# Second layer of a two-layer kernel: splits of transposed activations queued behind the next normalizations, and the last tiles' transposes behind their step's products

## The chip, the cores and the metric

One core of one Trainium2 chip runs the whole program. The core has five engines that run side by side, each in the order of its own instruction queue: PE (TensorE, matrix products), DVE (VectorE), ACT (ScalarE), POOL (GpSimd) and SP (SyncE, which here only issues DMAs). The metric is the device time in microseconds (us) of one execution; lower is better.

## What is computed

Attention over a window of 64 keys makes `x` (2304 tokens of 512 values); two layers follow. The change touches the second:

```python
h = x @ w_in                                  # 2304 x 512 times 512 x 1024
e = np.exp(h - h_max)
sm = e / (np.sum(e, axis=-1, keepdims=True) + 1e-09)
solu = h * sm
mu = np.mean(solu, axis=-1, keepdims=True)
var = np.mean((solu - mu) ** 2, axis=-1, keepdims=True)
ln = (solu - mu) / np.sqrt(var + 1e-06) * g_ln
return (ln @ w_out).astype(np.float32)        # 2304 x 1024 times 1024 x 512
```

## The kernel before

Every float32 operand of a product is held as two parts, hi and lo, and a product is three matmuls: hi with hi, hi with lo, lo with hi.

The second layer walks over 18 tiles of 128 tokens, t0 to t17. For a tile:

- `st_h2` (matmuls on L605): 24 matmuls of 512 columns make 1024 values a token in PSUM, tile `ps_h2`, of which there are three buffers.
- `st_ln`: the softmax-like unit and the normalization. The chain is DVE max (L616), ACT exponential (L617), three DVE steps (L618 to L620; L620 is the last to read `ps_h2`), DVE L621, ACT square with its sum (L622), DVE L623, POOL power (L624), DVE L628. The tiles `e` and `s` have two buffers each.
- `st_move`, all but the last three tiles: DVE transposes blocks of 32x32 (L638), SP writes the tile to DRAM (`lnd`, L639, 512 KB) and reads it back turned, in four pieces of 128 KB (`lT`, L641). A DRAM buffer is written and landed before it is read, so this is a round trip.
- `st_t2`: for both halves of the turned tile, ACT casts the hi part (`wih`, L662) and DVE subtracts it to get the lo part (`wil`, L663). The pair of casts and subtractions is called the splits here. The last three tiles (`DIRECT`) don't go through DRAM: PE turns them with 8 transposes (L657) into a `ps_h2` buffer and the splits read that.
- `st_out`: 24 matmuls (L674) into `ps_o` (two buffers), an ACT copy (L680), and a DMA out. The last tile does it in two halves of 256 columns.

`x2_split` makes hi and lo of the layer's input, three tiles at a time (ACT L525, DVE L526), from `x2r`, which a DMA of 768 KB loads (L516).

The loop runs 22 steps with `LAG = 4`: step i has the first product of tile i and the second of tile i-4. A scheduler then sorts each engine's instructions by its own estimate of time, so that the text order is a wish and not the queue's order; the instructions' dependencies and the order between calls named in the text are kept. In the text of before, `st_t2` of the last three tiles stands ahead of `st_out` of its step, and `st_t2` of the others stands at the end of the step with nothing that holds it back.

Below, "out k" is the second product of tile k, and "lnd k", "lT k" and "splits of k" go by tile in the same way.

Of the kernel before, what the change touches and what calls it, by code (L numbers as in the profile page):

```python
# [11 lines left out]
ACTF = mybir.ActivationFunctionType  # L12
ALU = mybir.AluOpType
# [7 lines left out]
def kernel(  # L21
# [12 lines left out]
    nc = tc.nc  # L34
# [63 lines left out]
    def as_f32(a):  # L98
        return a.bitcast(F32)
# [51 lines left out]
    def wtile(tag):  # L151
        return w_p.tile([128, 512], F32R, tag=tag, name=tag)
# [251 lines left out]
    def moe_g2(ps, u, hi, lo):  # L404
        g = nc.vector.tensor_tensor(u, ps, u, op=ALU.max)  # L405
        return nc.scalar.copy(hi, u).ins, g.ins  # L406
# [104 lines left out]
    NI = NT // 128  # L511
    x2h, x2l, x2raw = {}, {}, {}

    def x2_load(j):
        r = d_p.tile([128, KC, NB], F32, tag="x2", bufs=1, name="x2r")
        nc.sync.dma_start(out=r, in_=x2d[j].rearrange("e p n -> p e n"))  # L516
        x2raw[j] = r

    def x2_split(j, es):
        r = x2raw[j]  # L520
        if 0 in es:
            x2h[j] = wk_p.tile([128, KC, NB], F32R, tag="xh", name="x2h")
            x2l[j] = wk_p.tile([128, KC, NB], F32R, tag="xl", name="x2l")
        for e in es:
            nc.scalar.copy(x2h[j][:, e, :], r[:, e, :])  # L525
            nc.vector.tensor_tensor(  # L526
                x2l[j][:, e, :], r[:, e, :], as_f32(x2h[j][:, e, :]), op=ALU.subtract
            )
# [4 lines left out]
    for n in range(len(seq) + 2):  # L533
        if n < len(seq):
# [3 lines left out]
            if c == FIRST:  # L538
                z = na * (f + 1) // F0 - na * f // F0
# [18 lines left out]
        if n < len(seq):  # L558
# [3 lines left out]
            pins = moe_g2(*part)  # L562
# [32 lines left out]
    def st_h2(i):  # L595
        j, t = divmod(i, TPN)
        ps = ps2.tile([128, DF2], F32, tag="h2", bufs=3, name="ps_h2")
        tc_ = slice(t * 128, t * 128 + 128)
        for nn in range(2):
            cs = slice(nn * 512, nn * 512 + 512)  # L600
            n = 0
            for kc in range(KC):
                hi, lo = x2h[j][:, kc, tc_], x2l[j][:, kc, tc_]
                for a, w in ((hi, w2ih), (hi, w2il), (lo, w2ih)):
                    nc.tensor.matmul(ps[:, cs], a, w[kc, nn], start=(n == 0), stop=(n == 3 * KC - 1))  # L605
                    n += 1
        h2[i] = ps

    def st_ln(i):
        ps = h2.pop(i)  # L610
        e = d_p.tile([128, DF2], F32, tag="e", name="e")
        s = d_p.tile([128, DF2], F32, tag="s", name="s")
        l_ = s
        st = d_p.tile([128, 8], F32, tag="stat", name="stat")
        nmx, sm, rs, ssum, nmu, vs, rstd = (st[:, z:z + 1] for z in range(7))
        nc.vector.reduce_max(nmx, ps, axis=mybir.AxisListType.X, negate=True)  # L616
        nc.scalar.activation(e, ps, ACTF.Exp, bias=nmx, scale=1.0, accum_out=sm)  # L617
        nc.vector.tensor_scalar(sm, sm, 1e-9, None, op0=ALU.add)  # L618
        nc.vector.reciprocal(rs, sm)
        nc.vector.scalar_tensor_tensor(s, ps, rs, e, op0=ALU.mult, op1=ALU.mult, accum_out=ssum)  # L620
        nc.vector.tensor_scalar(nmu, ssum, -1.0 / DF2, None, op0=ALU.mult)  # L621
        nc.scalar.activation(e, s, ACTF.Square, bias=nmu, scale=1.0, accum_out=vs)  # L622
        nc.vector.tensor_scalar(vs, vs, 1.0 / DF2, 1e-6, op0=ALU.mult, op1=ALU.add)  # L623
        nc.gpsimd.tensor_tensor(rstd, vs, mhalf, op=ALU.pow)  # L624
        if i in DIRECT:
            l_ = e.rearrange("p (k b i) -> p b k i", b=4, i=32)
            s = s.rearrange("p (b k i) -> p b k i", b=4, i=32)
        nc.vector.tensor_scalar(l_, s, nmu, rstd, op0=ALU.add, op1=ALU.mult)  # L628
        ln[i] = l_, e

    def st_move(i):
        l_, lt = ln[i]
        if i not in DIRECT:
            lT = d_p.tile([128, 4, NK2, 32], F32, tag="st", bufs=NST, name="lT")
            nc.vector.transpose(lt, l_)  # L638
            nc.sync.dma_start(out=lnd[i], in_=lt)  # L639
            for a in range(4):  # L640
                nc.sync.dma_start(  # L641
                    out=lT[:, a].rearrange("p k j -> p (k j)"),
                    in_=lnd[i][32 * a:32 * a + 32, :].rearrange("i (b m) -> b i m", b=4),
                )
            ln[i] = lT

    def st_t2(i):
        lnh[i], lnl[i] = {}, {}
        l_ = ln.pop(i)
        for a in range(2):  # L650
            hi, lo = wtile(f"wih{8 + 2 * (i % 2) + a}"), wtile(f"wil{8 + 2 * (i % 2) + a}")
            lnh[i][a], lnl[i][a] = (z.rearrange("p (k t) -> p k t", t=128) for z in (hi, lo))
            if i in DIRECT:
                if a == 0:
                    ps = ps2.tile([128, DF2], F32, tag="h2", bufs=3, name="ps_t2")
                    for c in range(0, DF2, 128):
                        nc.tensor.transpose(ps[:, c:c + 128], l_[1][:, c:c + 128], ident)  # L657
                src = ps[:, 512 * a:512 * a + 512]
            else:
                src = l_[:, :, 4 * a:4 * a + 4, :].rearrange("p a k j -> p k a j")  # L660
                hi, lo = (z.rearrange("p (k a j) -> p k a j", k=4, a=4) for z in (hi, lo))
            nc.scalar.copy(hi, src)  # L662
            nc.vector.tensor_tensor(lo, src, as_f32(hi), op=ALU.subtract)  # L663


    def st_out(i):
        hi, lo = lnh.pop(i), lnl.pop(i)
        w = DM // 2 if i == NI - 1 else DM
        for c in range(0, DM, w):
            ps = ps2.tile([128, DM], F32, tag="o", name="ps_o")[:, 0:w]  # L670
            n = 0
            for kk in range(NK2):
                for a, b in ((hi, w2oh), (hi, w2ol), (lo, w2oh)):
                    nc.tensor.matmul(  # L674
                        ps, a[kk // 4][:, kk % 4, :], b[kk][:, c:c + w],
                        start=(n == 0), stop=(n == 3 * NK2 - 1),
                    )
                    n += 1
            o = d_p.tile([128, DM], F32, tag="o", name="o")[:, 0:w]
            nc.scalar.copy(o, ps)  # L680
            nc.sync.dma_start(out=out[i * 128:(i + 1) * 128, c:c + w], in_=o)

    LAG = 4
    for i in range(NI + LAG):
        if i < NI:
            st_h2(i)
        if i - 2 in DIRECT:
            st_t2(i - 2)  # L690
        if i >= LAG:
            st_out(i - LAG)
        if i < NI:
            st_ln(i)
            st_move(i)
            j, t = divmod(i, TPN)
            if t < 2 and j + 1 < NBLK:
                x2_split(j + 1, (2 * t, 2 * t + 1))
            if t == 2 and j + 2 < NBLK:
                x2_load(j + 2)  # L700
        for z in sorted(ln):
            if z <= i - LAG + 1 and z not in DIRECT:
                st_t2(z)


# [28 lines left out]
```

## Time and profile before

| | us |
|---|---|
| median of 3 runs | 748.56 |
| lowest and highest of them | 747.93 and 750.5 |
| the profiled execution | 749.73 |
| its span, first to last instruction | 747.9 |
| PE busy in it | 718.5 |
| DVE, ACT, POOL busy | 459.7, 355.1, 142.9 |

The profile is of one execution. The second layer's first matmul starts 530.74 us after the start of the span. A view that lists instructions gives start, duration, engine, line and operation, output and inputs, how many were merged, and in brackets how long the engine sat idle before and what it waited for. PE's matmuls overlap: the distance from start to start is their pace, not the duration shown.

### The profile page before, as it was taken

The numbers are of one execution on the slowest core, as the hardware profiler recorded it, in microseconds if no ns is written. First come the engines' busy times: TensorE is split into PE (matmuls) and PEld (weight loads), VectorE is DVE, ScalarE is ACT, GpSimd is POOL, SyncE is SP. The second block draws the span as 40 slices with busy tenths as digits, with TensorE's granted clock in tenths as the row PEclk, the third lists the DMA queues.
The fourth block names the chain that finished last, engine by engine and source line by source line (L and its number), as shares of the span: only waits on it lengthen the run. The fifth ranks groups of instructions, "written<-read, shape, count | busy, mean of one in ns | idle before, by whom it ended". The sixth has DMA issues, their size and how long they took to land. (4 is left out here: it accounts for less than half of the span.)

```text
span 747.9 us, 12383 instructions
## 1 busy us (share of the span) xinstructions
PE 718.5 (96%) x4321; PEld 657.4 (88%) x4321; DVE 459.7 (61%) x1208; ACT 355.1 (47%) x888; POOL 142.9 (19%) x167
## 2 busy tenths in 40 slices
PE   6899789999999999999999999999998999999988
PEld 5689778999999999999999999999886887788867
DVE  3559999576666666675567654534466546476550
ACT  5777765445445444545455443422342424444441
POOL 2459766101112111211112111100100000000000
PEclk9989999999999999999999999999998999999999
DMA  9996796524335534436342103860233333433311
GB/s 190 197 250 189 209 222 157 106 66 115 80 91 147 120 82 104 111 92 125 81 105 96 40 29 100 263 243 1 85 99 139 128 127 112 143 140 129 110 44 57
DMA packets 152598, 92.06 MB, mean 123 GB/s; under 512 B 117848, under 2 KB 137048, under 8 KB 152536
## 3 DMA queue, kind: packets, MB, share of 16 engines
q1 hardware_dynamic: 143320, 69.76, 35.9%
q0 software_dynamic: 9216, 21.51, 8.5%
q8 instruction: 34, 0.56, 0.3%
q14 instruction: 28, 0.23, 0.1%
HBM read 65.54 MB, written 25.69 MB: 122 GB/s over the span
## 5 line engine op out<-in xcount | busy, mean ns | idle before, releaser
L390 PE MATMUL ps_h<-xh,wih 128*128 128x384 f32 (+1 forms) x392 | 136.6, 349 | 2.7 <-DVE u L405 2.3
L390 PE MATMUL ps_h<-xh,wil 128*128 128x384 f32 (+1 forms) x392 | 134.0, 342 | 0.0
L390 PE MATMUL ps_h<-xl,wih 128*128 128x384 f32 (+1 forms) x392 | 132.7, 339 | 1.2 <-DVE xl L378 1.1
L421 PE MATMUL acc<-gh,woh 128*128 128x384 f32 (+1 forms) x392 | 131.0, 342 | 0.0
L421 PE MATMUL acc<-gl,woh 128*128 128x384 f32 (+1 forms) x392 | 130.9, 335 | 0.0
L421 PE MATMUL acc<-gh,wol 128*128 128x384 f32 (+1 forms) x392 | 130.5, 334 | 0.0
L400 ACT ACTIVATE u<-u,half 128x384 f32<-128x384 f32 (+1 forms) x98 | 59.6, 610 | 147.0 <-DVE u L399 146.7
L399 DVE TENSOR_SCALAR u<-ps_h 128x384 f32<-128x384 f32 (+1 forms) x98 | 53.5, 547 | 85.7 <-PE ps_h L390 85.6
L390 PEld LDWEIGHTS ps_h<-xh,wih 128*128 128x128 f32 x392 | 74.7, 191 | 5.1 <-DVE u L405 2.9
L390 PEld LDWEIGHTS ps_h<-xl,wih 128*128 128x128 f32 x392 | 74.9, 191 | 1.9 <-DVE xl L378 1.7
L390 PEld LDWEIGHTS ps_h<-xh,wil 128*128 128x128 f32 x392 | 75.0, 191 | 0.8
L421 PEld LDWEIGHTS acc<-gl,woh 128*128 128x128 f32 x392 | 74.2, 189 | 0.1
L421 PEld LDWEIGHTS acc<-gh,wol 128*128 128x128 f32 x392 | 74.0, 189 | 0.0
L421 PEld LDWEIGHTS acc<-gh,woh 128*128 128x128 f32 x392 | 73.5, 190 | 0.4
L406 ACT CAST gh<-u 128x384 fp32r<-128x384 f32 (+1 forms) x98 | 49.6, 506 | 50.3 <-DVE u L405 47.9
L405 DVE TENSOR_TENSOR u<-ps_h,u 128x384 f32<-128x384 f32 (+1 forms) x98 | 52.6, 536 | 33.9 <-ACT u L400 33.7
L674 PE MATMUL ps_o<-woh,wih 128*128 128x512 f32 (+1 forms) x152 | 59.8, 393 | 5.8 <-ACT wih L662 3.1
L135 POOL TENSOR_TENSOR w2st<-wst,w2st 128x512 fp32r<-128x512 f32 x16 | 20.9, 1309 | 227.6 <-ACT w2st L134 210.3
L317 ACT ACTIVATE p<-p,mx 128x128 f32<-128x128 f32 (+1 forms) x144 | 55.2, 385 | 8.5 <-DVE mx L311 8.3
L674 PE MATMUL ps_o<-wol,wih 128*128 128x512 f32 (+1 forms) x152 | 58.8, 387 | 0.0
L674 PE MATMUL ps_o<-woh,wil 128*128 128x512 f32 (+1 forms) x152 | 58.7, 386 | 0.0
L410 DVE TENSOR_TENSOR gl<-u,gh 128x384 fp32r<-128x384 f32 x80 | 44.2, 552 | 22.5 <-ACT gh L406 22.4
(93 smaller groups left out, 1277.8 us busy)
## 6 DMA issues: line engine op xcount, KB each, us to landing
vw<-in_v_dram SPq DMA_DIRECT2D x32, 256.0 KB
wst<-in_moe_w_in_dram SPq DMA_DIRECT2D x16, 512.0 KB
wst<-in_moe_w_out_dram SPq DMA_DIRECT2D x16, 512.0 KB
w2d<-w2st POOLq DMA_DIRECT2D x16, 512.0 KB, 3.4
lnd<-e SPq DMA_DIRECT2D x15, 512.0 KB
lT<-lnd SPq DMA_DIRECT2D x60, 128.0 KB
x2d<-xo POOLq DMA_DIRECT2D x24, 192.0 KB, 2.2
x2r<-x2d SPq DMA_DIRECT2D x6, 768.0 KB
```

The source lines that it names most:

```text
L135: nc.gpsimd.tensor_tensor(lo, val, as_f32(hi), op=ALU.subtract)
L317: nc.scalar.activation(p[:, i, c0:], tmp[:, i, c0:], ACTF.Exp, bias=mx[:, i:i + 1], scale=-1.0, accum_out=sm[:, i:i + 1],)
L390: nc.tensor.matmul(ps, a, bb[:, kc, c], start=(n == 0), stop=(n == 3 * KC - 1))
L399: nc.vector.tensor_scalar(u, ps, -1.0, 1.0, op0=ALU.max, op1=ALU.min)
L400: nc.scalar.activation(u, u, ACTF.Square, bias=half, scale=0.5)
L405: g = nc.vector.tensor_tensor(u, ps, u, op=ALU.max)
L406: return nc.scalar.copy(hi, u).ins, g.ins
L410: eng.tensor_tensor(lo, u, as_f32(hi), op=ALU.subtract)
L421: nc.tensor.matmul(acc[j, e][:, c], a, bb, start=(f == 0 and n == 0 and c.start == 0), stop=(f == NF - 1 and n == 2),)
L674: nc.tensor.matmul(ps, a[kk // 4][:, kk % 4, :], b[kk][:, c:c + w], start=(n == 0), stop=(n == 3 * NK2 - 1),)
```

## The change

```diff
-        nc.scalar.activation(e, s, ACTF.Square, bias=nmu, scale=1.0, accum_out=vs)
+        last_act = nc.scalar.activation(e, s, ACTF.Square, bias=nmu, scale=1.0, accum_out=vs).ins
...
-        nc.vector.tensor_scalar(l_, s, nmu, rstd, op0=ALU.add, op1=ALU.mult)
+        last_dve = nc.vector.tensor_scalar(l_, s, nmu, rstd, op0=ALU.add, op1=ALU.mult).ins
         ln[i] = l_, e
+        return last_act, last_dve
...
     LAG = 4
+    pins = []
     for i in range(NI + LAG):
         if i < NI:
             st_h2(i)
+        if i >= LAG:
+            st_out(i - LAG)
         if i - 2 in DIRECT:
             st_t2(i - 2)
-        if i >= LAG:
-            st_out(i - LAG)
         if i < NI:
-            st_ln(i)
+            pins.append(st_ln(i))
...
         for z in sorted(ln):
             if z <= i - LAG + 1 and z not in DIRECT:
-                st_t2(z)
+                act, dve = pins[min(i, NI) - 1 if i >= LAG else i]
+                with tc.issue_after(act), tc.issue_after(dve):
+                    st_t2(z)
```

`st_ln` hands back its last ACT instruction (the square, L622) and its last DVE instruction (L628). `issue_after` puts each instruction that its block records behind the one named, in the queue of that one's engine; it adds no semaphore. So the splits of a tile go behind the square and behind L628 of a later tile. The second edit writes `st_out` of a step ahead of the transposes of one of the last three tiles. No instruction is added or taken away; lines below the edits carry numbers one higher (L663 becomes L664). In the rows of order below, numbers behind a name tell buffers apart.

DVE at the start of the second layer, before. `lT_6303` is lT 0; `s_6342`, `s_6391` and `s_6438` are tiles 1, 2 and 3:

```order
L628 TENSOR_SCALAR s_6342<-s_6342,stat_6343 128x1024
L663 TENSOR_TENSOR wil8_6464<-lT_6303,wih8_6463 128x512
L663 TENSOR_TENSOR wil9_6468<-lT_6303,wih9_6467 128x512
L638 STREAM_TRANSPOSE e_6341<-s_6342 128x1024
L616 TENSOR_REDUCE stat_6439<-ps_h2_6412 128x1
L623 TENSOR_SCALAR stat_6392<-stat_6392 128x1
L628 TENSOR_SCALAR s_6391<-s_6391,stat_6392 128x1024
L638 STREAM_TRANSPOSE e_6390<-s_6391 128x1024
```

And DVE now, from the first splits on. `lT_6354` is lT 1; `stat_6526` and `stat_6611` belong to tiles 4 and 5:

```order
L628 TENSOR_SCALAR s_6438<-s_6438,stat_6439 128x1024
L664 TENSOR_TENSOR wil8_6464<-lT_6303,wih8_6463 128x512
L664 TENSOR_TENSOR wil9_6468<-lT_6303,wih9_6467 128x512
L664 TENSOR_TENSOR wil10_6549<-lT_6354,wih10_6548 128x512
L639 STREAM_TRANSPOSE e_6437<-s_6438 128x1024
L616 TENSOR_REDUCE stat_6611<-ps_h2_6556 128x1
L664 TENSOR_TENSOR wil11_6553<-lT_6354,wih11_6552 128x512
L526 TENSOR_TENSOR x2l_6713<-x2r_6629,x2h_6712 128x384 x4
L618 TENSOR_SCALAR stat_6526<-stat_6526 128x1
L619 RECIPROCAL stat_6526<-stat_6526 128x1
L618 TENSOR_SCALAR stat_6611<-stat_6611 128x1
L620 SCALAR_TENSOR_TENSOR s_6525,stat_6526<-ps_h2_6471,stat_6526,e_6524 128x1024
```

The splits of tile 0 moved from ahead of tile 1's transpose to behind tile 3's L628, those of tile 1 follow, and L620 of tile 4 now stands behind L618 of tile 5 (before, L618, L619 and L620 of tile 4 came with nothing of tile 5 between). In PE's queue this goes with a longer run of first products: before, out 0 started after t4, now after most of t6; then come the rest of t6, out 0, out 1, and out 2 between the matmuls of t7. From out 3 on, the two queues agree up to the last tiles.

DVE in the middle of the layer, before. `lT_6877` is lT 8, `s_7035` is tile 10:

```order
L620 SCALAR_TENSOR_TENSOR s_7035,stat_7036<-ps_h2_6981,stat_7036,e_7034 128x1024
L663 TENSOR_TENSOR wil8_7142<-lT_6877,wih8_7141 128x512
L621 TENSOR_SCALAR stat_7036<-stat_7036 128x1
L623 TENSOR_SCALAR stat_7036<-stat_7036 128x1
L663 TENSOR_TENSOR wil9_7146<-lT_6877,wih9_7145 128x512
L628 TENSOR_SCALAR s_7035<-s_7035,stat_7036 128x1024
L638 STREAM_TRANSPOSE e_7034<-s_7035 128x1024
```

And now, at the same tiles:

```order
L620 SCALAR_TENSOR_TENSOR s_7035,stat_7036<-ps_h2_6981,stat_7036,e_7034 128x1024
L621 TENSOR_SCALAR stat_7036<-stat_7036 128x1
L623 TENSOR_SCALAR stat_7036<-stat_7036 128x1
L628 TENSOR_SCALAR s_7035<-s_7035,stat_7036 128x1024
L664 TENSOR_TENSOR wil8_7142<-lT_6877,wih8_7141 128x512
L664 TENSOR_TENSOR wil9_7146<-lT_6877,wih9_7145 128x512
L639 STREAM_TRANSPOSE e_7034<-s_7035 128x1024
```

Both splits moved behind the normalization of tile 10 and ahead of its transpose. ACT's queue follows: before, its order was first cast, square, second cast, copy of `ps_o`; now it is square, both casts, copy.

PE at the end, before: the last matmul of t17's first product, tile 15's transposes, and out 13:

```order
L605 MATMUL ps_h2_7550<-wil7_5987,x2h_7222 128x512
L605 MATMUL ps_h2_7550<-wih7_5986,x2l_7223 128x512
L657 MATMUL ps_t2_7577<-ident_66,e_7455 128x128 x8
L674 MATMUL ps_o_7592<-woh0_5703,wih10_7542 128x512
L674 MATMUL ps_o_7592<-wol0_5704,wih10_7542 128x512
```

And now, where `ps_o_7575` is out 13 and `ps_o_7641` is out 14:

```order
L675 MATMUL ps_o_7575<-wol7_5991,wih11_7546 128x512
L675 MATMUL ps_o_7575<-woh7_5990,wil11_7547 128x512
L658 MATMUL ps_t2_7605<-ident_66,e_7455 128x128 x8
L675 MATMUL ps_o_7641<-woh0_5703,wih8_7633 128x512
L675 MATMUL ps_o_7641<-wol0_5704,wih8_7633 128x512
```

Each of the last three tiles' transposes moved behind one second product: tile 15's behind out 13, tile 16's behind out 14, tile 17's behind out 15.

## Rows read from the trace of the kernel before

**Rows 1.** Waits of PE, whole span: total us, times, longest us:
```profile
PE ps_o L674 <- ACT wih L662: 3.1, 1, 3.1
PE ps_t L657 <- DVE e L628: 2.9, 1, 2.9
...
PE ps_o L674 <- ACT o L680: 2.7, 2, 1.8
```
**Rows 2.** PE by stretches: length, busy (matmuls touched), granted clock, DMA share, GB/s:
```profile
558.14:580.67 22.53, 19.45 (x73) 0.85 0.33 120
...
596.99:665.95 68.96, 66.26 (x289) 1.00 0.37 127
665.95:709.48 43.53, 43.53 (x193) 1.00 0.36 128
709.48:727.73 18.25, 15.38 (x74) 0.91 0.14 52
```
**Rows 3.** Timeline of PE, soon after its first idle time of the layer:
```profile
573.42 0.63 PE L674 MATMUL ps_o<-woh,wil 128*128 128x512 f32 x1
573.84 0.63 PE L674 MATMUL ps_o<-woh,wih 128*128 128x512 f32 x1
```
**Rows 4.** Timeline of SP, DMA issues at the layer's start:
```profile
545.95 0.32 SPq L639 DMA_DIRECT2D lnd<-e  x1
548.68 2.29 SPq L641 DMA_DIRECT2D lT<-lnd  x4
551.15 0.38 SPq L516 DMA_DIRECT2D x2r<-x2d  x1
560.60 0.33 SPq L639 DMA_DIRECT2D lnd<-e  x1
563.23 2.17 SPq L641 DMA_DIRECT2D lT<-lnd  x4
565.50 0.48 SPq L639 DMA_DIRECT2D lnd<-e  x1
572.82 2.17 SPq L641 DMA_DIRECT2D lT<-lnd  x4
```
**Rows 5.** Groups by line from 480 us on: busy us, mean ns, idle before:
```profile
L620 DVE SCALAR_TENSOR_TENSOR s<-ps_h,stat,e 128x1024 f32<-128x1024 f32 x18 | 23.1, 1284 | 0.6
...
L622 ACT ACTIVATE e<-s,stat 128x1024 f32<-128x1024 f32 x18 | 20.7, 1150 | 16.0 <-DVE stat L621 16.0
L663 DVE TENSOR_TENSOR wil<-lT,wih 128x512 fp32r<-128x512 f32 x30 | 20.4, 691 | 39.4 <-ACT wih L662 39.3
L617 ACT ACTIVATE e<-ps_h,stat 128x1024 f32<-128x1024 f32 x18 | 20.1, 1117 | 46.2 <-issue 24.8 <-DVE stat L616 14.7 <-DVE s L628 3.6
L638 DVE STREAM_TRANSPOSE e<-s 128x1024 f32<-128x1024 f32 x15 | 18.7, 1244 | 0.3
```
**Rows 6.** Timeline of DVE, the first splits:
```profile
558.13 1.29 DVE L663 TENSOR_TENSOR wil<-lT,wih 128x512 fp32r<-128x512 f32 x2 [4.52 <-ACT wih L662]
```
**Rows 7.** Timeline of ACT around 652 us, in the middle of the layer:
```profile
651.16 0.62 ACT L662 CAST wih<-lT 128x512 fp32r<-128x512 f32 x1 [4.62 <-DMA lT<-lnd]
652.66 1.15 ACT L622 ACTIVATE e<-s,stat 128x1024 f32<-128x1024 f32 x1 [0.88 <-DVE stat L621]
...
654.32 0.57 ACT L680 COPY o<-ps_o 128x512 f32<-128x512 f32 x1
```
**Rows 8.** Timeline of SP in the middle, loads of turned tiles:
```profile
629.27 2.18 SPq L641 DMA_DIRECT2D lT<-lnd  x4
...
642.11 2.19 SPq L641 DMA_DIRECT2D lT<-lnd  x4
...
652.93 2.19 SPq L641 DMA_DIRECT2D lT<-lnd  x4
```
**Rows 9.** Chain that ended last, in order of time: start us, us, what:
```profile
713.98 0.63 ACT wih L662
...
718.83 1.94 PE ps_t L657 x8
```

## Prediction, made before the changed kernel ran

> **What bounds the kernel now.** PE is busy almost to the end, so I look for what it loses in the layer that the change touches. First the waits of PE [rows 1]: in the second layer it waits four times, 3.1 us for the casts of a turned tile, twice (2.7 us together) for the copy that frees a `ps_o` buffer, 2.9 us for the normalization ahead of tile 15's transposes. Then PE by stretches [rows 2]. The stretch from 665.95 is clean: 192 matmuls of 512 columns (the count includes one that only reaches in) in 43.53 us, 0.2267 us each, 5.44 us for a product of 24. Against that pace:
>
> - Start, 558.14 to 580.67: 72 matmuls are worth 16.32 us, the stretch took 22.53, lost 6.2. Only 3.1 of it is the wait; the rest is the clock, granted 0.85 on average. Matmuls start 0.42 us apart behind the wait [rows 3], that is at 1.2 in place of 2.4 GHz.
> - Middle, 596.99 to 665.95: 288 matmuls are worth 65.29, it took 68.96, lost 3.7, at clock 1.00.
> - Tail, 709.48 to 727.73: 49 matmuls and 24 transposes. Eight transposes at full clock take some 0.8 us, an estimate from their 128 of 512 columns and the start of a new kind of work, so 11.1 + 2.4 = 13.5 us; it took 18.25, lost 4.8, clock 0.91.
>
> The sum, 14.7 us of the 747.9 us span, is all that a reordering in this layer can win.
>
> Next, who is late. DVE stood idle 4.52 us ahead of the first splits [rows 6], since the splits of tile 0 stand in its queue and wait for the casts, and these for lT 0. The transpose of tile 1 is queued behind them, so the write lnd 1 goes out only at 560.60 [rows 4]. Over the layer DVE idles 39.4 us so [rows 5]. A wait of DVE is no loss by itself; it is one because the next tile's way through DRAM starts behind it.
>
> **Start of the layer.** The change takes the splits of tiles 0 and 1 behind tile 3's L628. DVE is then free at 553.6 (558.13 less 4.52 [rows 6]); it needs the square of tile 2, which ACT, no longer held by casts, starts at about 552.3 and ends 1.15 + 0.2 later, and transposes tile 1 until about 555.0 (1.24 [rows 5]). So lnd 1 is issued 5.6 us earlier than at 560.60.
>
> When does it land? With nothing else in flight, lnd 0 let its loads go 2.7 us after its issue [rows 4]: 557.7. But lT 0 (548.68) and the 768 KB of x2r (551.15) are in flight. lnd 2, issued at 565.50 behind lT 1, let its loads go only at 572.82: from one load to the next 9.6 us when the write hides behind the load [rows 4]. A round that held x2r as well took 12.8 against 10.8 for its neighbour [rows 8], 2.0 more. So lT 1 can go at 548.68 + 9.6 + 2.0 = 560.3; bounds are 557.7 and 561.5 (548.68 + 12.8). lT 2 follows 9.6 later at 569.9, and lnd 3 has landed 9.6 to 10.8 after that; I take 580.0.
>
> Now PE. In its new order it runs t5 (to 563.4 at the clean pace), 21 matmuls of t6, then the rest of t6 with out 0 and out 1: 72 x 0.2267 = 16.3 us, plus 0.3 for the cast of lT 1 (landed 8.8 after 560.3: lT 0 was cast at 558.13 less 0.62, 8.8 after its issue [rows 4, 6]), to 580.0. Nothing waits there: tile 3's L620 is over 2.9 us after lnd 1's landing (L617 1.12 and its read-out 0.2, two small steps, L620 1.28 [rows 5]), that is at 563.2. The wait of 3.1 is gone.
>
> What is late next: t7 needs the `ps_h2` buffer of tile 4, free after tile 4's L620. That now stands behind L618 of tile 5, which needs L617 of tile 5, which writes the `e` buffer that lnd 3 reads. So it ends 2.9 to 3.0 us after lnd 3's landing, at 583.0, and PE is idle 3.0 us from 580.0. Then it can do only nine products up to 587.2: ACT has square, two casts and a copy to do before out 2, DVE another L620 (1.28), L628 and one split (0.69). Nine are worth 2.0 us, so 2.2 more are lost. The idle time is as long as the one before (3.1), so I expect the low clock again; part of it falls in the waits just named, so I take 1.0 us for it, from bounds of 0 and 3.1 (its cost at the start of before, 6.2 less the wait). Together 0.3 + 3.0 + 2.2 + 1.0 = 6.5 against 6.2: the start gets 0.3 us **worse**, between 4 better (landing at 557.7 shifts all by 2.6 and leaves an idle time as short as the middle's, which kept the clock at 1.00 [rows 2]) and 3 worse.
>
> A rule speaks against this stall. The Trainium skill, page "DMA: Bandwidth & Descriptors", section "Anatomy of one DMA — SWDGE (gpsimd) path", fits a DMA's time as 2.0 us plus its bytes over 436 GB/s, for another issuing engine. That gives 3.2 us for the 512 KB of a turned tile, where this case's rows show 8.7; by the page lnd 3 would land before PE arrives at t7, the 6.5 us would go, and the total would be near 734. The row decides.
>
> **Middle.** At the wait that ends at 654.9, lT 8 landed at 651.16 [rows 7]. Then the first cast, the split on DVE, only then L621 of tile 10 behind it, the square from 652.66, the second cast, and the copy of `ps_o` to 654.89, for which PE waited: 3.7 us after the landing. In the new order L621 and the square are over before, so both casts (0.62 and 0.5) and the copy (0.57) are done at 652.9, where PE had waited till 654.9. The longest of the two waits was 1.8, the gain is 2.0: they vanish even if no load lands earlier. And loads should land earlier: lT 3 goes at 580.0, out 3 starts at 597.3 (0.3 after the end of the stretch before). With an x2r in the next round (12.8), lT 4 lands at 580.0 + 12.8 + 8.7 = 601.5, and out 4 wants it at 608.2: 6.7 us ahead. DVE's transpose of tile i now stands behind both splits of tile i-2, but that is only 0.6 + 2 x 0.7 + 1.24 = 3.2 us after a landing, while the next load is still in flight for 5 us: hidden; without that cover it would cost 3.2 a round. Gain 3.7, bounds 0 and 3.7.
>
> **Tail.** In the trace of before PE waits for the normalization of tile 16, which stands behind splits of lT 14, cast at 713.98; PE starts the transposes at 718.83 [rows 9]. Now L628 of tile 16 stands ahead of those splits, and the transposes behind one more product of 5.44 us: covered twice. The later links, counted from the end of t17: out 13 and tile 15's transposes are through at 6.2; a cast 0.6, L617 of t17 1.3 (now queued behind that cast), small steps 0.5, L620 1.3 and a split 0.7 bring tile 15's splits to 10.6, wanted after out 14 and tile 16's transposes at 12.4; square, power and L628 of t17, some 3.3 more, end at 13.9, wanted after out 15 at 17.9. Nothing waits, so the low clock goes too: gain 4.8, bounds 3 and 4.8. The last copy and the last DMA are as before.
>
> **Sum.** +0.3 - 3.7 - 4.8 = -8.2 us, on the profiled execution 749.73 to 741.5 (its span to 739.7). That execution lies 1.2 above the median of 748.56, so for the median I say **740.4**.
>
> **Rivals.**
> - *Short rounds at the start* (0.10): lnd 1 is not held by what is in flight and lands at 557.7. PE's second wait shrinks to some 0.4 us and the clock holds: 4 better, 736.4. For it: lnd 0 took 2.7. Against: lnd 2 behind lT 1. The page named above points this way.
> - *Only the tail gains* (0.13): the middle's 3.7 stays, because DMA rounds with x2r and output writes land too late whatever the order: 744.1. For it: 12.8 against PE's 10.88 a step [rows 8]. Against: 10.8 next to it, and 2.0 us won on the engines alone.
> - *The start eats the gain* (0.09): both rounds up to lnd 3 take 12.8, not 9.6 and 10.1, so it lands at 586, PE idles 6 us more and pays the whole low clock (1.9): 748.3.
> - *Slower* (0.05): the round through DRAM becomes the bound, since the transpose of tile i now waits for the landing of i-2. If all ten rounds from lT 4 to lT 14 took 12.8, 2.0 more than PE's 10.88 each, 20 us less the lead of 6.7 come on top: 753.5. It turns slower than before from a mean round of about 12.6 (10.88 plus a tenth of 6.7 + 8.2 + 2.2). The neighbour's 10.8 and the start's 9.6 speak against it.
>
> **How the numbers follow.** Forecast 0.63, its own range 738.5 to 743. What a measurement can tell from no change is 0.3%, 2.2 us, so faster means below 746.3: 0.63 + 0.10 + 0.13 = 0.86; within, 0.09; slower, 0.05. The range runs from 736 to 745: it takes in the short rounds and the tail alone, and leaves the last two cases and a little at each end out.
>
> **What would show it.** Start: lnd 1 issued near 555, the next load near 560; one idle time of PE of about 3 us near 580 ahead of t7, ended by DVE's L620. An idle time near 572 would mean that the order did not do what it says; none near 580, short rounds. Middle: no wait of PE for a copy at 613 to 655, and DVE's waits for casts standing right behind L628. Tail: no wait ahead of the transposes, clock 1.00 from 600 on. I am wrong if PE loses more than 10 us at the start, or if it waits for casts in the steady part.

## The result, and the profile after

| | before | after |
|---|---|---|
| median of 4 runs each | 748.43 us | 740.30 us |
| lowest and highest | 747.93 and 750.5 | 739.77 and 740.36 |
| profiled execution (its span) | 749.73 (747.9) | 740.36 (738.6) |
| second layer, PE's first to last instruction | 213.7 | 206.3 |

The ratio is 0.9885, with a 95% interval from 0.9865 to 0.9904: 8.1 us faster, by the medians. The forecast was 740.4. Of the 9.3 us between the two spans, 2.0 lie ahead of the second layer (it starts at 528.77, in the trace of before at 530.74), in code that did not change, and 7.4 lie in the layer. In the traces of this document the layer starts anywhere from 527.60 to 530.74, so the 2.0 can't be put down to the change.

The waits of PE in the second layer, after (total us, times, longest us), answer to [rows 1]:

```profile
PE ps_h L605 <- DVE stat L619: 2.2, 1, 2.2
...
PE ps_o L675 <- ACT o L681: 0.8, 1, 0.8
...
PE ps_h L605 <- DVE s L620: 0.4, 1, 0.4
```

The wait for casts (3.1), both waits for copies ahead of the tail (2.7) and the one for the normalization (2.9) are gone. A new one of 2.2 stands in their place, ahead of t7, with one of 0.8 behind it, ahead of out 2, and one of 0.4 before it, where t6 waits for tile 3's L620 (562.01).

PE by stretches, after (length, busy, matmuls touched, granted clock, DMA share, GB/s), against [rows 2]; the first four lines follow one another, the last two cut the layer where out 3 starts:

```profile
558.14:580.67 22.53, 20.36 (x88) 1.00 0.27 97
580.67:597.30 16.63, 15.39 (x55) 0.79 0.57 185
597.30:702.00 104.70, 104.70 (x463) 1.00 0.36 124
702.00:734.90 32.90, 32.90 (x181) 1.00 0.19 67
528.77:595.92 67.15, 63.74 (x265) 0.95 0.37 125
595.92:735.10 139.18, 139.17 (x649) 1.00 0.31 110
```

And the same cut at out 3 in the trace of before:

```profile
530.74:597.00 66.26, 63.18 (x265) 0.95 0.33 113
597.00:744.43 147.43, 141.86 (x649) 0.99 0.31 110
```

That is the whole result in four numbers. Up to out 3 the layer got 0.9 us longer (66.26 to 67.15). From out 3 on it got 8.25 shorter, and there PE is now busy in all of its 139.18 us, at clock 1.00 and at the clean pace (the 19 products from out 3 to t17 take 103.36 us, 5.44 each): nothing is left to win there but by fewer or shorter matmuls.

What is left stands ahead of out 3. All engines after, around the new wait (start, duration, engine, what ran, in brackets the idle time before and what ended it):

```profile
578.30 2.17 SPq L642 DMA_DIRECT2D lT<-lnd  x4
...
578.38 1.11 ACT L617 ACTIVATE e<-ps_h,stat 128x1024 f32<-128x1024 f32 x1 [6.92 <-DMA lnd<-e]
...
579.62 0.15 DVE L618 TENSOR_SCALAR stat<-stat 128x1 f32<-128x1 f32 x1 [5.72 <-ACT e L617]
579.69 1.27 DVE L620 SCALAR_TENSOR_TENSOR s<-ps_h,stat,e 128x1024 f32<-128x1024 f32 x1
...
581.12 0.47 PE L605 MATMUL ps_h<-wih,x2h 128*128 128x512 f32 x1 [2.16 <-DVE stat L619]
```

Read upwards from the last line. t7 waits for the `ps_h2` buffer of tile 4, so for tile 4's L620 at 579.69. That was ready long before, but DVE's queue has L618 of tile 5 ahead of it; L618 waits for L617 of tile 5 on ACT, which waits (6.92 us of idle ACT) for lnd 3 to land, since it writes the `e` buffer that lnd 3 reads. lT 3 is issued at the same moment, 578.30. The view of the waits names L619, a small step behind in the queue; the timeline shows which instruction it really is.

SP's queue after, at the layer's start, against [rows 4]:

```profile
546.72 2.29 SPq L642 DMA_DIRECT2D lT<-lnd  x4
549.18 0.37 SPq L516 DMA_DIRECT2D x2r<-x2d  x1
552.97 0.33 SPq L640 DMA_DIRECT2D lnd<-e  x1
558.86 2.17 SPq L642 DMA_DIRECT2D lT<-lnd  x4
561.14 0.50 SPq L640 DMA_DIRECT2D lnd<-e  x1
568.62 2.17 SPq L642 DMA_DIRECT2D lT<-lnd  x4
```

lnd 1 went out 24.2 us after the layer's start, in before 29.9. But its loads followed 5.9 us later (558.86), in before 2.6: part of the earlier start was eaten by the 768 KB of `x2r` in flight.

The tail held, but narrowly. All engines after, ahead of out 14:

```profile
708.00 1.14 ACT L663 CAST wih<-lT 128x512 fp32r<-128x512 f32 x2 [2.45 <-DMA lT<-lnd]
...
709.04 0.58 ACT L681 COPY o<-ps_o 128x512 f32<-128x512 f32 x1
...
710.17 1.04 PE L658 MATMUL ps_t<-ident,e 128*128 128x128 f32 x8
...
710.96 0.48 PE L675 MATMUL ps_o<-woh,wih 128*128 128x512 f32 x1
```

out 14 starts at 710.96 and writes the buffer that this copy (of out 12) frees. out 12 itself was over at 699.3, but its copy stands on ACT behind the casts of lT 14. It ends at 709.62, 1.3 us before it is needed.

### The profile page after: what moved, and what is told of

It reads as the page before. It is cut to its first block, busy times and chain, and to the rows that moved or that the text cites. A ratio compares the mean times of both kernels' runs of the same rounds, so it can differ in the third digit from the quotient of the medians.

```text
span 738.6 us, 12378 instructions
## 1 busy us (share of the span) xinstructions
PE 713.7 (97%) x4321; PEld 653.4 (88%) x4321; DVE 460.1 (62%) x1208; ACT 355.5 (48%) x888; POOL 142.8 (19%) x167
## 4 chain that ended last, share of the span: by engine, by line
PE 84%; DVE 5%; DMA 5%; issue 2%; ACT 1%; SPq 1%; POOL 1%; DVEq 0%; ACTq 0%; POOLq 0%
PE ps_h L390 26%; PE acc L421 25%; PE ps_o L675 12%; PE ps_h L605 9%; PE ps_s L303 5%; PE ps_x L370 3%; PE ps_p L351 2%; DMA lnd<-e 2%; DMA wst<-in_moe_w_in_dram 1%; DMA lT<-lnd 1%; DVE wst L125 1%; PE ps_t L285 1%; DMA wst<-in_moe_w_out_dram 1%; DVE s L620 1%; DVE e L639 0%
## 5 line engine op out<-in xcount | busy, mean ns | idle before, releaser
L605 PE MATMUL ps_h<-wih,x2h 128*128 128x512 f32 x144 | 56.6, 393 | 2.6 <-DVE stat L619 2.2
```

## The experiments

Times are medians; the ratios are to the kernel before, run beside each set. That one stood between 748.3 and 749.5 in the three sets, so the ratios compare better than the times. "Layer" is from the second layer's first matmul to PE's last, of the profiled execution, one each: it leaves the first stage out, which varied by some 3 us from trace to trace.

### The two edits apart

The tie alone, with the transposes ahead of `st_out` as before (shown against the changed kernel):

```diff
-        if i >= LAG:
-            st_out(i - LAG)
         if i - 2 in DIRECT:
             st_t2(i - 2)
+        if i >= LAG:
+            st_out(i - LAG)
```

> The changed kernel without its second edit: the splits are tied behind the normalizations, but the last tiles' transposes stand ahead of their step's second product, as before. Theory (each edit alone is enough for the tail, since the tie puts tile 16's L628 ahead of the splits of lT 14): PE does not wait in the tail, and the time is that of the changed kernel, 740.3 us, within 1.0. Rival (the two edits add up, the tail belongs to the move of the transposes): the tail's 4.8 us comes back, 745.0 us.

Measured: 742.15 us, ratio 0.9909 (0.9888 to 0.9929); layer 209.3: between the two expectations, nearer to the theory in time, but what happened is the rival's: the tail's loss is back. The order and the waits of the start are much as in the changed kernel, and so is the middle: every product between 594 and 703 takes 5.44. From t17's start to the end it takes 40.6 us, in the changed kernel 35.8 (699.28 to 735.10), in the kernel before 40.4 (704.03 to 744.43). The total lost less than that, because in this trace the clock held behind the wait at t7 (last section): out 3 starts 65.3 us after the layer's start, in the changed kernel 67.15. The timeline of the tail:

```profile
715.80 1.15 ACT L622 ACTIVATE e<-s,stat 128x1024 f32<-128x1024 f32 x1 [2.00 <-DVE stat L621]
...
717.41 0.58 ACT L681 COPY o<-ps_o 128x512 f32<-128x512 f32 x1
...
718.05 0.51 PE L675 MATMUL ps_o<-woh,wih 128*128 128x512 f32 x1 [1.72 <-ACT o L681]
...
719.11 1.06 PE L658 MATMUL ps_t<-ident,e 128*128 128x128 f32 x8 [0.55 <-DVE e L628]
```

Now tile 17 is the late one: PE waits for a copy behind its square (L622), then for its L628.

The other edit alone, the order of the transposes without the tie:

```diff
-                act, dve = pins[min(i, NI) - 1 if i >= LAG else i]
-                with tc.issue_after(act), tc.issue_after(dve):
-                    st_t2(z)
+                st_t2(z)
```

> The changed kernel without its first edit: the transposes stand behind their step's product, the splits are free as before. Theory: the start and the middle are as before (6.2 and 3.7 us lost), the tail is clean, 748.4 - 4.8 = 743.6 us. Rival (the tail's wait only moves one product further, because tile 16's normalization is held by lT 14 all the same): 747 to 748.5 us.

Measured: 746.75 us, ratio 0.9962 (0.9948 to 0.9976); layer 213.5: nearer to the rival in time, between the two by the ratio. Start and middle are those of before. The layer of this trace is only 0.2 us shorter than that of before, so the 2.8 us by which the median is lower are not explained by it. In the tail:

```profile
712.82 0.62 ACT L663 CAST wih<-lT 128x512 fp32r<-128x512 f32 x1 [3.48 <-DMA lT<-lnd]
...
715.47 0.60 ACT L663 CAST wih<-lT 128x512 fp32r<-128x512 f32 x1
...
715.98 1.06 ACT L681 COPY o<-ps_o 128x512 f32<-128x512 f32 x2
...
716.61 0.80 PE L675 MATMUL ps_o<-woh,wih 128*128 128x512 f32 x1 [2.27 <-ACT o L681]
```

The transposes no longer wait (they run at 713.30, right behind out 13). The wait moved on by one product: out 14 waits for copies that stand behind both casts of lT 14. From t17's start to the end it takes 39.9 us (702.41 to 742.27). So neither edit clears the tail alone: each leaves some 4 to 5 us there, about as much as before, and only the two together take it away. The middle is the tie's alone.

### What is left at the start

A third `e` buffer, so that L617 of tile 5 need not wait for lnd 3:

```diff
-        e = d_p.tile([128, DF2], F32, tag="e", name="e")
+        e = d_p.tile([128, DF2], F32, tag="e", bufs=3, name="e")
```

> The changed kernel with three buffers of the tile e in place of two, so that the exponential of tile 5 need not wait for the landing of the write of tile 3. Theory (this buffer holds L620 of tile 4, and that holds PE at t7): PE's wait of 2.2 us near 579 and most of the low clock behind it go, 734 to 736 us. Rival (the round through DRAM itself is late, the buffer only happens to be in the way): PE waits as long, now for the casts of tile 2, 739.5 to 740.5 us.

Measured: 742.63 us, ratio 0.9910 (0.9893 to 0.9926); layer 208.2. The cause of the wait is confirmed: it is gone, and out 3 starts 61.6 us after the layer's start in place of 67.15. But the time did not fall, and the total was missed. PE's waits in this kernel's second layer:

```profile
PE ps_o L675 <- ACT o L681: 4.8, 3, 3.0
...
PE ps_o L675 <- ACT wih L663: 1.5, 2, 1.2
...
PE ps_o L675 <- DVE wil L664: 0.6, 1, 0.6
```

The two longest come at 646 (1.5) and 710 (3.0), each for a copy that stands behind the casts of a turned tile. Counted from the layer's start, lT 14 was issued at 172.2 us, in the changed kernel at 170.9: PE arrived 5.5 us earlier, the loads did not. That was not expected, and the later runs are about it.

The load of `x2r` that held lnd 1, issued later:

```diff
-                x2_load(j + 2)
+                if j == 1:
+                    with tc.issue_after(writes[3]):
+                        x2_load(j + 2)
+                else:
+                    x2_load(j + 2)
```

(`writes[i]` is the DMA that writes tile i, L640.)

> The changed kernel with the load of x2r for tiles 9 to 11 queued on SP behind the write of tile 3, where it stood ahead of the write of tile 1. Theory (the write of tile 1 lands behind the x2r in flight): the first load of tile 1 is issued 2.7 to 3.0 us after the write in place of 5.9, each later round 3 us earlier, and PE's wait at t7 shrinks to under 0.5 us: 735 to 737 us. Rival (the write is held by the load of tile 0, not by x2r): still 5 us or more from write to load, 739.5 to 740.5 us.

Measured: 737.23 us, ratio 0.9836 (0.9818 to 0.9855); layer 203.2. SP's queue there:

```profile
551.80 0.32 SPq L640 DMA_DIRECT2D lnd<-e  x1
555.00 2.17 SPq L642 DMA_DIRECT2D lT<-lnd  x4
```

With no `x2r` in flight the loads follow the write after 3.2 us, not 5.9. The wait ahead of t7 is gone. Two waits for copies are left, 2.6 us ahead of out 2 and 1.0 in the tail.

### Copies ahead of casts

The splits also tied behind the copy of the product that ended last, so that a copy need not stand behind a cast that waits for a load. Three kernels, with the changed kernel again beside them:

```diff
-            nc.scalar.copy(o, ps)
+            freed[i] = nc.scalar.copy(o, ps).ins
...
-                with tc.issue_after(act), tc.issue_after(dve):
+                last = freed.get(i - LAG - 1, act)
+                with tc.issue_after(act), tc.issue_after(dve), tc.issue_after(last):
```

> The changed kernel once more, unaltered, so that the other three stand beside it on one chip. 741 us, ratio to the kernel before 0.989. Its trace should again show one idle time of PE of about 2.2 us ahead of t7. Open is whether the clock falls behind it, as it did in the first trace (0.79 for 16.6 us), or holds, as it did in the kernel with the tie alone after idle times of 2.26 and 1.32 us: if the fall is chance, the two executions will differ by about 2.4 us at the start of the layer.

Measured: 739.45 us, ratio 0.9873 (0.9853 to 0.9894); layer 206.4, the same wait of 2.2 ahead of t7, and the low clock behind it again.

> The changed kernel, and the splits also tied behind ACT's copy of the second product that ended last, so that a finished copy no longer stands behind a cast that waits for a load. Theory (what is left of the danger in the changed kernel is copies queued behind casts): the 0.8 us that PE waits for a copy at the start goes, the idle time ahead of t7 stays, the tail has no wait as before; 740 us, 1 below the changed kernel, ratio 0.988. Rival (the order of ACT there doesn't matter, or L617 of the next tile is now held behind a copy that waits for PE): 741 to 744, with new waits of PE for L620 in the steady part.

Measured: 740.20 us, ratio 0.9879 (0.9861 to 0.9897). The time is the theory's, but it is no gain on the changed kernel beside it: the wait for a copy ahead of out 2 (1.0 there) became one for the cast (1.5). The rival's first reason, that ACT's order there doesn't matter, fits; its 741 to 744 and its waits for L620 in the steady part did not come.

> The kernel with the late x2r load, and the same tie behind the copy. With the late load alone PE waited 2.56 us ahead of out 2 and 1.04 us in the tail for a copy that stood on ACT behind casts. Theory (the order on ACT made these waits): both go, 737.2 - 3.6 = 733.6 us, ratio 0.979. Rival (the casts are late themselves, so that PE waits for them in place of the copies): 737 us, no change against the late load alone.

Measured: 737.77 us, ratio 0.9851 (0.9832 to 0.9871). A miss for the theory; the rival's 737 fits. The tail's wait went, but ahead of out 2 PE waits as long as before, for the cast:

```profile
580.18 1.15 ACT L622 ACTIVATE e<-s,stat 128x1024 f32<-128x1024 f32 x1
...
581.33 0.56 ACT L681 COPY o<-ps_o 128x512 f32<-128x512 f32 x1
581.79 1.14 ACT L663 CAST wih<-lT 128x512 fp32r<-128x512 f32 x2
...
582.46 0.50 PE L675 MATMUL ps_o<-woh,wih 128*128 128x512 f32 x1 [2.51 <-ACT wih L663]
```

The cast came late itself, as the rival had it. lT 2 was there at about 574.7 by estimate (issued at 565.97, and lT 1 of the changed kernel took 8.7 us from issue to cast), but the ties put its casts behind the square of tile 4 and a copy, and that square stood behind L617 of tile 5, which waits for lnd 3.

> As the kernel with the late load and the tie behind the copy, and a third e buffer. Theory (what is left at the layer's start is L617 waiting for the e buffer that a write to DRAM still reads): PE's idle time ahead of t7 is gone and no more than 1 us can be won on the kernel without the third buffer, 733 us. Rival (as with the third buffer alone, PE gets ahead of the rounds through DRAM and waits for copies and casts later): 734 to 737, with waits of 3 us or more in sum between 640 and 715.

Measured: 739.36 us, ratio 0.9877 (0.9858 to 0.9897): outside both. In its trace the start has the same wait for the cast (2.4) with the low clock, and the tail one of 0.6. With the wait at t7 gone already, a third `e` buffer gave nothing that the runs show (its interval overlaps that of the kernel without it).

### Two causes, taken away one by one

So two things held the start: L617 of a tile ahead of the square of the tile before on ACT, and loads of `x2r` ahead of writes on SP. The first, from tile 5 on:

```diff
-        nc.scalar.activation(e, ps, ACTF.Exp, bias=nmx, scale=1.0, accum_out=sm)
+        with tc.issue_after(pins[-1][0]) if i > 4 else nullcontext():
+            nc.scalar.activation(e, ps, ACTF.Exp, bias=nmx, scale=1.0, accum_out=sm)
```

> The changed kernel, and from t5 on each exponential (L617) tied behind the square (L622) of the tile before, so that the normalization of tile 4 no longer stands behind the exponential of tile 5, which waits for the landing of lnd 3. Both theories expect PE's idle time of 2.2 us ahead of t7 and the low clock behind it to go, and out 3 to start some 61.5 us after the layer's start in place of 67.2. Theory A (only PE's losses count): the 5 us stay, 735 us, ratio 0.981. Theory B (the rounds through DRAM are a second bound: in the kernel with the third e buffer lT 14 went at 699.83 though out 3 started 5.5 us earlier, in the changed kernel at 699.62): lT 14 is issued 170.5 to 171.5 us after the layer's start as before, PE waits some 3 us for copies or casts ahead of out 14 and 15, 738.5 to 740.5 us, ratio 0.986 to 0.988.

Measured: 740.56 us, ratio 0.9897 (0.9880 to 0.9914); layer 206.4: no gain, so theory A is out, and the time lies just above theory B's range. But the loss is not in the place that B named: the tail has no wait. The wait ahead of t7 is gone, t7 and out 2 run without one, and then:

```profile
591.46 2.19 SPq L642 DMA_DIRECT2D lT<-lnd  x4
591.48 1.11 ACT L617 ACTIVATE e<-ps_h,stat 128x1024 f32<-128x1024 f32 x1 [5.19 <-DMA lnd<-e]
...
592.59 1.12 ACT L663 CAST wih<-lT 128x512 fp32r<-128x512 f32 x2
...
593.25 0.80 PE L675 MATMUL ps_o<-woh,wih 128*128 128x512 f32 x1 [3.14 <-ACT wih L663]
```

The casts for out 3 stand behind L617 of tile 6, which waits for lnd 4, and lnd 4 was issued at 583.00 behind the next `x2r`. out 3 had started 67.15 us after the layer's start, and it starts 64.4 after it here, but the low clock behind this wait takes all of that back (142.1 from there to the end, in place of 139.2). lT 14 went 169.7 us after the layer's start, a little ahead of the 170.5 that I expected.

The second: all three loads of `x2r` in the layer behind writes.

```diff
-                x2_load(j + 2)
+                with tc.issue_after(writes[{1: 3, 2: 5, 3: 8}[j]]) if j else nullcontext():
+                    x2_load(j + 2)
```

> The changed kernel, with all three loads of x2r in the layer tied on SP behind writes of turned tiles (lnd 3, lnd 5, lnd 8) instead of ahead of lnd 1, lnd 4 and lnd 8. In the changed kernel these three rounds took 12.1, 12.7 and 13.4 us from load to load, the others about 10.6. Theory B: the two later rounds shrink too, to 10.9 or below, lT 14 goes 166 to 168 us after the layer's start (169.2 with only the first load moved), the tail's wait of 1.0 us for a copy goes; 735.5 to 736.5 us, ratio 0.982. Theory A: nothing on the kernel with only the first load moved, ratio 0.9836.

Measured: 737.71 us, ratio 0.9857 (0.9836 to 0.9878); layer 203.8: above the 736.5 of theory B, and at best what theory A had, nothing on the kernel with one load moved (0.9836). The rounds shrank as expected (lT 14 at 165.1 us after the layer's start; the tail is clear). The time did not follow, since the start kept its wait of 2.9 ahead of out 2, this time with the low clock (0.88 from 583.14 to 597.00).

> Both: exponentials behind the square before, and the three loads behind writes. PE's stalls at the start go and the rounds leave room. Theory B: out 3 starts 60.5 to 61.5 us after the layer's start, the rest takes 139.2 to 140, the layer 200 to 201.5 us against 206.3; 733.5 to 735 us, ratio 0.980. Rival (the rounds cannot follow a start that is 6 us earlier even so): waits of 2 us or more for casts or copies between 640 and 715, 737 us.

Measured: **734.87 us**, ratio 0.9818 (0.9803 to 0.9832); layer 200.4, out 3 61.2 us after its start. All as theory B put it. PE's only wait left in the layer, and PE cut at out 3 as above:

```profile
PE ps_o L675 <- ACT o L681: 1.0, 1, 1.0
```
```profile
529.61:590.80 61.19, 60.19 (x266) 1.00 0.33 112
590.80:729.97 139.17, 139.17 (x649) 1.00 0.35 121
```

> As the kernel with both, and the splits tied behind the copy of the product that ended last. If the copies still stand behind casts somewhere, this wins up to 1 us, 733 us; with the casts late in place of the copies, as when this tie was added to the kernel with one late load, it is the same or up to 1 us slower.

Measured: 735.53 us, ratio 0.9827 (0.9810 to 0.9843). With both causes gone the tie behind the copy adds nothing.

By the medians, and against the changed kernel's two ratios (0.9885 and 0.9873), the tie on ACT alone gives nothing, the three loads alone 1 to 2 us with intervals that overlap, both together 4 to 5. The layers of the traces say the same: 206.4, 203.8 and 200.4 us. The traces show why: each cause stood behind the other. The kernel with both beats the changed one by the gap of two intervals that do not touch (0.9803 to 0.9832 against 0.9853 to 0.9904 in its two measurements). Its interval overlaps that of the kernel with one load moved (0.9818 to 0.9855), so what it gains on that one rests on the two traces alone (layers of 200.4 and 203.2).

## Why the prediction was right, point by point

**Start: +0.9, forecast +0.3.** Direction and mechanism held, the terms did not. Counted from the layer's start, lnd 1 was forecast at 24.3 us and went at 24.2; lT 1 at 29.6 and went at 30.1; t7's wait should end at 52.3 and ended at 52.35. The cause that was named, L620 of tile 4 behind L618 of tile 5 behind lnd 3, is the one in the timeline, and two kernels that took it away (a third `e` buffer; the square first) lost that wait. The terms inside the sum were off both ways. PE's idle time was 2.2, not 3.0, since PE came to t7 some 0.8 later than forecast; half of that is the wait of 0.4 ahead of t6, for tile 3's L620, where the prediction says "Nothing waits there". The wait ahead of out 2 was 0.8, not 2.2. The clock cost about 3, not 1.0: between 581.12 and 595.92 the 48 matmuls are worth 10.9 us at the clean pace and took 14.8, and 0.8 of the rest is the wait. Starts 0.42 to 0.43 us apart show 1.2 in place of 2.4 GHz, as in [rows 3]. The term for the clock had bounds of 0 and 3.1; it came out at the upper one. That these errors nearly cancel is luck, and so is the clock itself: with the tie alone it held behind the same waits, and out 3 came 1.8 us sooner.

**The landing of lnd 1.** The choice that mattered was 560.3 against 557.7, "held by what is in flight". The trace gave 5.9 us from write to load, the forecast 5.3; with the `x2r` moved it was 3.2. So the `x2r` in flight was the cause, and the rival *short rounds* priced its absence near the mark: 736.4 in the text (736.1 by its own terms), 737.2 in the run with the load moved. It did so in part by luck, since it had a wait of 0.4 at t7, and the run has none there but 2.6 us ahead of out 2, with the clock at 1.00. The Trainium skill, page "DMA: Bandwidth & Descriptors", section "Anatomy of one DMA — SWDGE (gpsimd) path", gives a fit for one DMA of another issuing engine; the estimate from it for the 512 KB of a turned tile is 3.2 us. The trace after does not agree either: lT 1 was issued at 558.86 and cast at 567.56, 8.7 us later. (For the kernel before the prediction says 8.7 too; its rows give 8.8 [rows 4, 6] and 9.05 [rows 7, 8].)

**Middle: -3.7.** Held, and shown to be the tie's work: the kernel with the tie alone has no wait there, the one without it has all of them (0.8 and 1.6 for copies). The reason given for it ("both casts and the copy are done at 652.9") is not tested apart from the earlier loads: lT 8 was cast 115.6 us after the layer's start (644.41), in the kernel before 120.4 (651.16), so 4.8 us of the room come from the load and not from ACT's order.

**Tail: -4.8.** Right in its sum: middle and tail together were forecast at 8.5 and gave 8.25; cut at t17's start, 3.7 and 4.6. Wrong in one phrase, "covered twice". It was meant as two edits, either of which would do. The two runs with one edit each left 4 to 5 us in the tail. The tie makes tile 16's normalization early, the move of the transposes gives tile 17's time to end; the move without the tie only hands the wait to the copy behind the casts of lT 14. And the margin is 1.3 us, not a product of 5.44. The forecast counted the links of DVE and PE, and left out that out 14 needs the copy of out 12, which ACT has behind those casts.

**The rounds through DRAM.** The rival *slower* was kept at 0.05 because rounds of 12.8 would have to be the rule. From lT 4 to lT 14 the mean was 10.87 (590.97 to 699.62, ten rounds), PE's own 10.88: they did not slow the kernel. But they were close to being a second bound, with a pace of their own: between 590 and 700, SP waits 75.5 us for landings of written tiles and 1.4 for DVE. That is why taking the wait at t7 away won nothing with the third `e` buffer, where PE waited for casts and copies later. With the square first it was a single round, the one of 12.9 us that held an `x2r`, which made the casts for out 3 late. And it pays once the rounds are shorter too (10.6 in the mean in the fastest kernel, 587.44 to 693.59). The three rounds that held an `x2r` took 12.1, 12.7 and 13.4 us, the others 9.6 to 11.1; behind a write in place of ahead of it, they took 10.3, 10.9 and 11.0.

**The total.** 740.4 against 740.30 is closer than the terms deserve. In the traces the layer got 7.4 us shorter, not 8.2, and the rest of the difference lies in the stage ahead, which varies by more than that. Two more prices of rivals are off by 0.2 by their own terms (*slower* 753.7, not 753.5; *the start eats the gain* 748.5, with 2.1 for the whole low clock in place of 1.9); nothing hangs on them.

## What to carry to other kernels

An instruction that waits for a DMA blocks what stands behind it in its engine's queue, so put the work that others wait for (buffer-freeing copies, normalizations) ahead of it, and look where the next such instruction stands: here taking one away showed another one tile further on. Read the slack as well as the waits: a kernel that is clean from 597 us to its end had 1.3 us left ahead of out 14, and a gain upstream of a loop with its own pace (here rounds through DRAM) can be lost as long as that loop is no shorter, as with the third `e` buffer. A large load that is not urgent goes behind the small write that is.

## What was not expected of the hardware

The low clock does not follow from the length of the idle time alone. Two kernels with nearly the same idle times at the same place, the changed one (2.16 and 0.79 us) and the one with the tie alone (2.26 and 1.32), granted clocks of 0.77 and 1.00 behind them. PE in the same 48 matmuls, t7 to out 3, first of the changed kernel, then of the tie alone:

```profile
581.12:595.92 14.80, 14.01 (x48) 0.77 0.62 200
```
```profile
581.50:594.24 12.74, 11.42 (x48) 1.00 0.58 188
```

The changed kernel did the same in its second trace. A wait of 2.56 ahead of out 2 kept the clock in one kernel (the late load), one of 2.51 in nearly the same place did not (late load and copies first). In the tail, a wait of 2.27 ahead of out 14 was followed by 0.87 over 12.4 us (the move alone), and one of 3.04 there kept the clock (third `e` buffer, from that wait on):

```profile
710.17:722.00 11.83, 10.87 (x49) 1.00 0.18 66
```

What decides behind idle times of 2 to 3 us stays open; it is worth up to 3 us a time here, as much as the waits themselves.
